# Reordering the first loads of a sketched-attention and four-expert kernel: keys in two runs a row, values in eight pieces, expert weights and query rows moved between them

## The chip, the cores and the metric

One core of a Trainium2 chip. A time is the device time in microseconds (us) of one execution; a kernel's time is the median of its runs. Every run in this study was in the fast state. A profile is of one of those runs, and its span is about 1.8 us shorter than the time of the same run (485.9 against 487.64 for the kernel before).

## The reference, cut to what matters

Attention with sketched keys and queries (each row is multiplied with two 8 x 32 matrices S1 and S2, and the products of the two results are its features), then four experts over every row.

```python
def phi(x):                                   # q, k, v: (4, 4, 1088, 32)
    a = np.einsum('rd,bhsd->bhsr', S1, x)     # S1, S2: (8, 32)
    b = np.einsum('rd,bhsd->bhsr', S2, x)
    return np.einsum('bhsi,bhsj->bhsij', a, b).reshape(*x.shape[:-1], 64)

q_p, k_p = phi(q), phi(k)
kv = np.einsum('bhsf,bhsd->bhfd', k_p, v)     # needs ALL keys and values of a batch
z = np.sum(k_p, axis=2)
out = einsum(q_p, kv) / (einsum(q_p, z) + 1e-06)
x = out as (4352, 128)
y = sum over e of p[:, e] * (relu(x @ w1[e]) @ w2[e])   # w1: (4,128,1024), w2: (4,1024,128)
```

The dependence that matters here: no attention output, and so no expert matmul, before the sum over all keys and values of batch 0 is complete, the last value tile included.

## The kernel before

Each DMA here is one load. `load_rows` fetches rows of k or q as 128 partitions, `load_v` fetches the values in four pieces of 32 partitions and then the 33rd and 34th rows (the "last value tile", two loads of 16 KB).

```python
def load_v(b):
    t = lpool.tile([P, H * NT * D], F32, tag="vn", name="vn")
    ...
    for a in range(4):                        # 4 x 128 KB, 32 partitions each
        nc.sync.dma_start(_ap(t, 32 * a, 32, 0, [[8 * D, H], [1, 8 * D]]), ...)
    for a in range(2):                        # the last value tile: 2 x 16 KB
        nc.sync.dma_start(_ap(t, 32 * a, 32, 1024, [[D, H], [1, D]]), ...)
    return t
...
load_rows(k, 0, "kn")                         # 544 KB, one load
load_rows(q, 0, "qn", slice(0, P))            # 64 KB
vn[0] = load_v(0)
...
load_rows(q, 0, "qn", slice(P, S))            # 480 KB
load_w1(0)                                    # 512 KB
# ... gate rows (dp, ends), w2(0), then w1 and w2 of experts 1 to 3
...
keep_warm(11)                                 # matmuls on constants, 0.43 us apart
```

In the part of `start` that the argument needs, ScalarE copies the values into the layout of the sums (`vx`), tile after tile, and only then copies `qb`, which the query products need:

```python
def value_copy(b):
    for r in range(2):
        nc.scalar.copy(vx[:, 4*r : 4*r+4, ...], _ap(vn[b], 0, P, P * r, ...))
        yield
    nc.scalar.copy(vx[0:64, 8, :, 0:D], _ap(vn[b], 0, 64, 1024, ...))   # the last tile

# in start():
    key_project(b, 0, kf[0]); key_project(b, 1, kf[1])
    next(value)
    key_project(b, 2, kf[2])
    for _ in value:                           # second copy, then the last tile
        pass
    ...
    nc.scalar.copy(qb[:, 0:n], fq[0][:, 0:n])
    # key products, key sums, query products, kvz, attention of the first rows, experts
```

Two facts count later, and the trace of the kernel before shows both. Only eight loads are under way at once: each load waits for the landing of the load eight before it in program order (the rest of q was issued at 4.95, the keys, eight loads before it, had landed at 4.93). And ScalarE runs its copies in program order (the second copy of values at 8.56, the last tile's at 9.09, qb's at 9.29).

Of the kernel before, what the change touches and what calls it, by code (L numbers as in the profile page):

```python
# [8 lines left out]
F32 = mybir.dt.float32  # L9
# [3 lines left out]
ACTF = mybir.ActivationFunctionType  # L13
# [3 lines left out]
def _ap(t, p0: int, np_: int, off: int, free):  # L17

    p = list(t.ap)[0]
    return bass.AP(t.tensor, t.offset + p0 * p[0] + off, [[p[0], np_]] + [list(d) for d in free])  # L20
# [3 lines left out]
def kernel(  # L24
# [24 lines left out]
    nc = tc.nc  # L49

    P = 128
    HP = 64
    B, H, S, D = q.shape
    E, DM, F = w1.shape
    R = 8
    R2 = 2 * R
    G = S // 32
    assert (B, H, S, D) == (4, 4, 1088, 32) and (E, DM, F) == (4, P, 1024)
    NT = 9
# [6 lines left out]
    UNITS = [[P, 448, 512], [512, 320, 256], [448, 512, P], [384, 320, 384]]  # L66
# [6 lines left out]
    cpool = ctx.enter_context(tc.tile_pool(name="const", bufs=1))  # L73
    lpool = ctx.enter_context(tc.tile_pool(name="loads", bufs=1))
# [9 lines left out]
    def psum(pool, tag):  # L84
        return pool.tile([P, 512], F32, tag=tag, name=tag)


    def load_rows(src, b, name, part=slice(0, S)):

        d = kn if name == "kn" else qn  # L90
        if b not in d:
            d[b] = lpool.tile([P, S], F32, tag=name, bufs=2, name=name)
        c, n = part.start, part.stop - part.start
        base = src.offset + b * H * S * D
        if name == "qn" and b == B - 1:
            for c, n, t in ((0, (G - 4) * D, 0), ((G - 4) * D, 4 * D, S - P)):
                nc.sync.dma_start(d[b][:, c : c + n], bass.AP(src.tensor, base + t * D, [[S * D, H], [n, 32], [1, n]]))
        else:
            nc.sync.dma_start(d[b][:, part], bass.AP(src.tensor, base + c, [[G * D, P], [1, n]]))

    def load_v(b):
        t = lpool.tile([P, H * NT * D], F32, tag="vn", name="vn")
        base = v.offset + b * H * S * D
        for a in range(4):
            nc.sync.dma_start(
                _ap(t, 32 * a, 32, 0, [[8 * D, H], [1, 8 * D]]),
                bass.AP(v.tensor, base + 8 * a * D, [[G * D, 32], [S * D, H], [1, 8 * D]]),
            )
        for a in range(2):
            nc.sync.dma_start(  # L110
                _ap(t, 32 * a, 32, 1024, [[D, H], [1, D]]),
                bass.AP(v.tensor, base + (32 + a) * D, [[G * D, 32], [S * D, H], [1, D]]),
            )
        return t

    kn, qn, vn = {}, {}, {}

    def load_batch(b):
        load_rows(k, b, "kn")
        vn[b] = load_v(b)  # L120
        load_rows(q, b, "qn")

    s_raw = cpool.tile([R2, 2 * D], I32, name="s_raw")
# [5 lines left out]
    def load_w1(e):  # L129
        nc.sync.dma_start(w1_sb[:, e, :], w1[e])  # L130

    def load_w2(e):
        nc.sync.dma_start(w2_sb[:, e], w2[e].rearrange("(f p) d -> p f d", p=P))

    load_rows(k, 0, "kn")
    load_rows(q, 0, "qn", slice(0, P))
    vn[0] = load_v(0)


    warm = nc.const_aps.tensor(1.0, (P, 512), BF16)  # L140

    idle = cpool.tile([P, 1], F32, name="idle")
    nc.scalar.activation(idle[:, :], nc.const_aps.tensor(1.0, (P, 1), F32), ACTF.Identity)
    dp = cpool.tile([P, G, E], F32, name="dp")

    ends = cpool.tile([P, 2, E], F32, name="ends")
    e_sum = cpool.tile([P, 2, 3], F32, name="e_sum")
    load_rows(q, 0, "qn", slice(P, S))
    load_w1(0)
    for p0, n, g0, m, t in ((0, 96, 0, G, 0), (96, 32, 0, G - 4, 3 * S), (96, 32, G - 4, 4, B * S - P)):  # L150
        nc.sync.dma_start(
            _ap(dp, p0, n, g0 * E, [[1, m * E]]),
            bass.AP(domain_probs.tensor, domain_probs.offset + t * E, [[m * E, n], [1, m * E]]),
        )
    for i, t, g in ((0, 0, G), (1, B * S - P, 4)):
        nc.sync.dma_start(
            ends[:, i, :], bass.AP(domain_probs.tensor, domain_probs.offset + t * E, [[g * E, 32], [1, 4 * E]])
        )
    load_w2(0)
    for e in range(1, E):  # L160
        load_w1(e)
        load_w2(e)
    sk = cpool.tile([P, P], F32, name="sk")
# [22 lines left out]
    def keep_warm(n):  # L186

        for _ in range(n):
            wp = psum(ps_h, "h")
            nc.tensor.matmul(wp[:, :], warm[:, 0:P], warm[:, :], start=True, stop=True)  # L190

    keep_warm(11)


    turn = [0]
# [130 lines left out]
    def key_turn(b, r, t0=0, n=4):  # L326
        if r < 2:
            nc.vector.transpose(  # L328
                _ap(kT, 0, P, 512 * r + P * t0, [[P, n], [32, 4], [1, 32]]),
                _ap(kn[b], 0, P, P * r + 32 * t0, [[32, n], [8 * D, 4], [1, 32]]),  # L330
            )
        else:
            nc.vector.transpose(kT[:, 1024:S], kn[b][:, 1024:S])
# [98 lines left out]
    def keys(b):  # L432
        for r in range(3):
            key_turn(b, r)
            yield
        kf = []
        for gi, (pool, tag) in enumerate(((ps_f, "f"), (ps_n, "den"), (ps_n, "num"))):
            kf.append(psum(pool, tag))
            key_project_wide(b, gi, kf[gi])
            if gi:  # L440
                key_add(b, gi - 1, kf[gi - 1])
            yield
        for _ in value_copy(b):
            pass
        for t0, n in ((0, 4), (4, 5)):
            if t0:
                key_add(b, 2, kf[2])
            for p in range(2):
                for x in range(2):
                    key_product(b, t0, n, p, x, nc.vector)  # L450
# [3 lines that stand above are left out]
        kv = psum(ps_f, "f")  # L454
        for p in range(2):
            key_sum(b, p, kv)
            yield
        key_blocks(b, kv)
        yield
# [214 lines left out]
    def start():  # L674
# [4 lines left out]
        for t0 in (0, 2):  # L679
            key_turn(b, 0, t0, 2)  # L680
        for r in (1, 2):
            key_turn(b, r)
# [52 lines left out]
    def front():  # L735
        for b in range(B):
            if b:
                yield from keys(b)
                if b + 1 < B:
                    load_batch(b + 1)  # L740
            c = 0
            for n in UNITS[b]:
                if b or c:
                    yield from queries(b, c, n)
                c += n
# [230 lines left out]
    for i in range(len(steps) + LA):  # L976
        if i < len(steps):
# [21 lines left out]
            if i == 2:  # L999
                gate_quotients()  # L1000
            elif i == 5:
                store_gates()
                load_gate(1)
                load_gate(2)
                load_batch(1)
# [43 lines left out]
```

## Time and profile before

| | kernel before |
|---|---|
| median time | 488.02 us (487.82 to 488.66, 3 runs) |
| span of the profile | 485.9 us |
| TensorE busy | 99% |
| first expert matmul (moment F) | 13.2 us |
| last piece of v landed | 7.66 us |
| last value tile landed | 8.06 us |
| w1 of expert 0 landed | 11.20 us |

Landings are read from the trace's DMA records; a load has landed when the last of its engines has finished. The kernel is bound by TensorE from F to the end (busy for 469.70 of the 469.70 us from 13.16 to 482.86), so the only time to be had is in front of F. The prediction below shows the lines for that. One line is added, because the explanation will rest on it: the stretch from 5 to 8 us, in which the values come in. Columns: stretch, length, busy time and count of TensorE, weight loads, VectorE, ScalarE and GpSimd, then granted clock, DMA share, GB/s.

```profile
5.00:8.00 3.00, 2.64 (x80) 2.48 (x81) 2.40 (x7) 1.40 (x5) 1.45 (x5) 1.00 1.02 229
```

The DMA engines are busy all through (share 1.02), at 229 GB/s.

### The profile page before, as it was taken

How to read it: one execution, taken by the hardware profiler on the slowest of the kernel's cores; microseconds unless marked ns; L12 is line 12 of the kernel's file. 1: busy time of each engine (PE TensorE's matmuls, PEld its weight loads, DVE VectorE, ACT ScalarE, POOL GpSimd, SP SyncE). 2: the span in 40 equal slices, each digit the busy share in tenths (PEclk: the TensorE clock that was granted, in tenths of full speed). 3: DMA queues.
4: the chain of work that ended last, by engine and by line, in shares of the span. 5: the costliest groups of instructions: out<-in, count | busy, mean ns of one | idle time of the engine just before them, and what ended most of it. 6: DMA issues, size and time to landing. Idle time of an engine off the chain costs nothing.

```text
span 485.9 us, 11377 instructions
## 1 busy us (share of the span) xinstructions
PE 481.5 (99%) x4551; PEld 362.7 (75%) x4551; DVE 320.9 (66%) x759; ACT 246.8 (51%) x496; POOL 230.0 (47%) x270
## 2 busy tenths in 40 slices
PE   8999999999999999999999999999999999999997
PEld 6965666667777777777777777677777777999997
DVE  6859675686766668486776757668684666665642
ACT  4354564445544555355445555445455555566651
POOL 5172654435444455415455444424555445555571
PEclk9999999999999999999999999999999999999999
DMA  7990050211003123031103100021101200120001
GB/s 223 278 299 10 23 150 12 88 20 45 2 9 106 24 69 93 2 89 20 40 1 130 24 12 1 3 86 24 34 0 56 50 1 0 45 55 4 15 1 20
DMA packets 37772, 26.25 MB, mean 54 GB/s; under 512 B 24824, under 2 KB 34520, under 8 KB 37208
## 3 DMA queue, kind: packets, MB, share of 16 engines
q1 hardware_dynamic: 37704, 25.53, 18.9%
q8 instruction: 36, 0.59, 0.5%
q14 instruction: 16, 0.13, 0.1%
q10 hardware_dynamic: 16, 0.00, 0.0%
HBM read 21.28 MB, written 4.24 MB: 53 GB/s over the span
## 4 chain that ended last, share of the span: by engine, by line
PE 97%; DMA 1%; DVE 1%; issue 0%; SPq 0%; ACT 0%; ACTq 0%
PE h L202 50%; PE o L202 41%; PE f L202 3%; PE den L202 2%; DMA kn<-in_k_dram 1%; PE num L202 1%; DVE qp L501 0%; DVE kp L391 0%; DVE kT L328 0%; DVE qT L488 0%; SPq L125 0%; DVE end L856 0%; DVE kvz L414 0%; ACT fs L360 0%; ACT vx L337 0%
## 5 line engine op out<-in xcount | busy, mean ns | idle before, releaser
L202 PE MATMUL h<-xT,w_sb 128*64 128x512 f32 (+5 forms) x1424 | 300.2, 491 | 0.0
L786 DVE SCALAR_TENSOR_TENSOR hid<-h,hid 128x256 f32<-128x256 f32 (+6 forms) x432 | 203.7, 472 | 143.3 <-ACT hid L817 134.9
L817 ACT ACTIVATE hid<-h 128x512 f32<-128x512 f32 (+3 forms) x288 | 158.5, 550 | 192.3 <-PE h L202 146.2
L202 PE MATMUL o<-hid,w2s 128*64 128x256 f32 (+3 forms) x1152 | 224.0, 355 | 0.0
L202 PEld LDWEIGHTS h<-xT,w_sb 128*64 128x64 f32 x1424 | 147.5, 137 | 50.4 <-issue 6.4
L202 PE MATMUL o<-hid,w_sb 128*64 128x256 f32 (+3 forms) x864 | 183.7, 355 | 0.0
L202 PEld LDWEIGHTS o<-hid,w2s 128*64 128x64 f32 x1152 | 132.2, 137 | 28.9
L930 POOL TENSOR_TENSOR ev<-yz,sh 64x256 f32<-64x256 f32 (+3 forms) x72 | 48.7, 676 | 159.9 <-ACT sh L933 157.2
L202 PEld LDWEIGHTS o<-hid,w_sb 128*64 128x64 f32 x864 | 100.5, 137 | 25.2 <-issue 5.8
L918 POOL TENSOR_TENSOR yz<-ev 128x512 f32<-128x512 f32 (+3 forms) x36 | 41.7, 1160 | 60.4 <-ACT ev L921 60.2
L930 POOL TENSOR_TENSOR ct<-ev 128x512 f32<-128x512 f32 (+3 forms) x36 | 42.5, 1182 | 2.8
L930 POOL TENSOR_TENSOR total<-total,ct 128x512 f32<-128x512 f32 (+3 forms) x27 | 31.9, 1181 | 2.1
L930 POOL TENSOR_TENSOR ct<-ct,gate 128x512 f32<-128x512 f32 (+3 forms) x27 | 31.8, 1177 | 2.1
L501 DVE TENSOR_TENSOR qp<-qa,qb 64x512 f32<-64x512 f32 (+5 forms) x44 | 30.1, 685 | 1.0
L920 ACT COPY ev<-o 128x512 f32<-128x512 f32 (+3 forms) x36 | 19.4, 539 | 12.7 <-PE o L202 12.3
L202 PE MATMUL o<-w_sb,hid 128*64 128x128 f32 x256 | 22.3, 273 | 0.0
L921 ACT COPY ev<-o 128x512 f32<-128x512 f32 (+3 forms) x36 | 19.4, 539 | 2.0
L202 PEld LDWEIGHTS o<-w_sb,hid 128*64 128x64 f32 x256 | 18.1, 137 | 1.6 <-issue 0.9
L809 ACT ACTIVATE hid<-h 128x256 f32<-128x256 f32 x23 | 8.4, 384 | 18.3 <-PE h L202 17.9
L391 DVE TENSOR_TENSOR kp<-fs 128x256 f32<-128x256 f32 (+1 forms) x24 | 16.6, 696 | 0.1
L933 ACT COPY sh<-yz 64x256 f32<-64x256 f32 (+3 forms) x36 | 13.7, 380 | 1.7 <-POOL yz L918 0.8
L202 PEld LDWEIGHTS den<-kvx,qp 128*64 128x64 f32 x240 | 12.5, 137 | 2.5 <-issue 0.5
(129 smaller groups left out, 247.5 us busy)
## 6 DMA issues: line engine op xcount, KB each, us to landing
w_sb<-in_moe_w_dram SPq DMA_DIRECT2D x8, 512.0 KB, 5.8
gate<-gates SPq DMA_DIRECT2D x4, 1024.0 KB, 4.7
kn<-in_k_dram SPq DMA_DIRECT2D x4, 544.0 KB, 7.0
vn<-in_v_dram SPq DMA_DIRECT2D x16, 128.0 KB, 3.5
gate<-gates SPq DMA_DIRECT2D x2, 896.0 KB, 6.4
qn<-in_q_dram SPq DMA_DIRECT2D x2, 544.0 KB, 4.0
out_dram<-ob SPq DMA_DIRECT2D x16, 64.0 KB, 2.0
qn<-in_q_dram SPq DMA_DIRECT2D x2, 480.0 KB, 5.0
```

Of the source, the lines that this page charges most:

```text
L202: nc.tensor.matmul(out(s), weights(s), moving(s), **flags)
L391: eng.tensor_tensor(out=_ap(kps[b], 0, P, 256 * t0 + P * p + 64 * x, [[256, n], [32, 2], [R, 4], [1, R]]), in0=_ap(src, 0, P, off + 4 * x, ...
L501: nc.vector.tensor_tensor(out=qp[p][64 * x : 64 * x + 64, 0:n], in0=qa[64 * p : 64 * p + 64, 0:n], in1=qb[64 * p : 64 * p + 64, 0:n], op=A ...
L786: nc.vector.scalar_tensor_tensor(out=out, in0=src, scalar=0.0, in1=in1, op0=ALU.max, op1=ALU.subtract)
L809: nc.scalar.activation(hd[:, 0 : 2 * n], hp[:, 0 : 2 * n], ACTF.Relu)
L817: nc.scalar.activation(hd[:, n * j : n * j + n], hp[:, 0:n], ACTF.Relu)
L918: add = lambda out, in0, in1, op=ALU.add: nc.gpsimd.tensor_tensor(out=out, in0=in0, in1=in1, op=op)
L920: nc.scalar.copy(_ap(ev, 0, P, 0, [[2 * w, 2], [1, w]]), _ap(a0, 0, P, 0, two))
L921: nc.scalar.copy(_ap(ev, 0, P, w, [[2 * w, 2], [1, w]]), _ap(a1, 0, P, 0, two))
L930: add = lambda out, in0, in1, op=ALU.add: nc.gpsimd.tensor_tensor(out=out, in0=in0, in1=in1, op=op)
L933: nc.scalar.copy(sh[HP:P, 0:w], yz[0:HP, 0, 0:w])
```

## The change

Intent: let the first half of the keys land early so that TensorE starts on them sooner; cut the values so that the first half of every row lands first; issue two of the loads from ScalarE; and fetch the first experts' weights sooner, as they are wanted next. All arithmetic stays the same. The core of the diff:

```diff
-    load_rows(k, 0, "kn")
-    load_rows(q, 0, "qn", slice(0, P))
-    vn[0] = load_v(0)
+    for part in (slice(0, 512), slice(512, S)):
+        load_rows(k, 0, "kn", part)               # 256 KB, 288 KB
+    v_tile(0)
+    for a in range(4):
+        load_v(0, 0, a)                           # 64 KB each
+    load_rows(q, 0, "qn", slice(0, P), nc.scalar) # issued by ScalarE
+    load_v(0, 1, 0, nc.scalar)                    # issued by ScalarE
+    for a in range(1, 4):
+        load_v(0, 1, a)
+    load_w1(0)
+    load_rows(q, 0, "qn", slice(P, P + UNITS[0][1]))   # 448 columns, 224 KB
+    load_v_end(0)                                 # the last value tile
+    load_w2(0)
...
-    load_rows(q, 0, "qn", slice(P, S))
-    load_w1(0)
     # ... dp
+    load_w1(1)
     # ... ends
-    load_w2(0)
-    for e in range(1, E):
+    load_w2(1)
+    load_rows(q, 0, "qn", slice(P + UNITS[0][1], S))
+    for e in range(2, E):
...
-    keep_warm(11)
+    keep_warm(9)
...
-                _ap(kn[b], 0, P, P * r + 32 * t0, [[32, n], [8 * D, 4], [1, 32]]),
+                _ap(kn[b], 0, P, 512 * r + 32 * t0, [[32, n], [P, 4], [1, 32]]),
```

The last hunk reads the keys in another order, so that the first half of the key tiles needs only the first run. The sum over keys does not care about the order, but values must follow it: that is why v is cut in eight.

More of the change, by code (lines that the diff above doesn't have):

```diff
@@ L85, in psum, with load_rows @@
         return pool.tile([P, 512], F32, tag=tag, name=tag)
-    def load_rows(src, b, name, part=slice(0, S)):
+    def load_rows(src, b, name, part=slice(0, S), engine=nc.sync):
         d = kn if name == "kn" else qn
@@ L98, in load_rows, with v_tile, load_v, load_v_end @@
         else:
-            nc.sync.dma_start(d[b][:, part], bass.AP(src.tensor, base + c, [[G * D, P], [1, n]]))
-    def load_v(b):
-        t = lpool.tile([P, H * NT * D], F32, tag="vn", name="vn")
-        base = v.offset + b * H * S * D
-        for a in range(4):
-            nc.sync.dma_start(
-                _ap(t, 32 * a, 32, 0, [[8 * D, H], [1, 8 * D]]),
-                bass.AP(v.tensor, base + 8 * a * D, [[G * D, 32], [S * D, H], [1, 8 * D]]),
-            )
+            engine.dma_start(d[b][:, part], bass.AP(src.tensor, base + c, [[G * D, P], [1, n]]))
+    def v_tile(b):
+        vn[b] = lpool.tile([P, H * NT * D], F32, tag="vn", name="vn")
+    def load_v(b, r, a, engine=nc.sync):
+        engine.dma_start(
+            _ap(vn[b], 32 * a, 32, P * r, [[8 * D, H], [1, P]]),
+            bass.AP(v.tensor, v.offset + (b * H * S + 16 * r + 4 * a) * D, [[G * D, 32], [S * D, H], [1, P]]),
+        )
+    def load_v_end(b):
         for a in range(2):
             nc.sync.dma_start(
-                _ap(t, 32 * a, 32, 1024, [[D, H], [1, D]]),
-                bass.AP(v.tensor, base + (32 + a) * D, [[G * D, 32], [S * D, H], [1, D]]),
+                _ap(vn[b], 32 * a, 32, 1024, [[D, H], [1, D]]),
+                bass.AP(v.tensor, v.offset + (b * H * S + 32 + a) * D, [[G * D, 32], [S * D, H], [1, D]]),
             )
-        return t
     kn, qn, vn = {}, {}, {}
@@ L119, in load_batch @@
         load_rows(k, b, "kn")
-        vn[b] = load_v(b)
+        v_tile(b)
+        for r in range(2):
+            for a in range(4):
+                load_v(b, r, a)
+        load_v_end(b)
         load_rows(q, b, "qn")
@@ L133, in load_w2 @@
         nc.sync.dma_start(w2_sb[:, e], w2[e].rearrange("(f p) d -> p f d", p=P))
-    load_rows(k, 0, "kn")
-    load_rows(q, 0, "qn", slice(0, P))
-    vn[0] = load_v(0)
-    warm = nc.const_aps.tensor(1.0, (P, 512), BF16)
     idle = cpool.tile([P, 1], F32, name="idle")
     nc.scalar.activation(idle[:, :], nc.const_aps.tensor(1.0, (P, 1), F32), ACTF.Identity)
+    for part in (slice(0, 512), slice(512, S)):
+        load_rows(k, 0, "kn", part)
+    v_tile(0)
+    for a in range(4):
+        load_v(0, 0, a)
[7 more added lines that the diff above has]
+    load_w2(0)
+    warm = nc.const_aps.tensor(1.0, (P, 512), BF16)
     dp = cpool.tile([P, G, E], F32, name="dp")
```

## The prediction

> **What bounds the kernel now.** I read the page's busy shares first, then the same shares cut into three stretches, then the chain of work that ended last for the first 14 us, then ScalarE's timeline there, then the DMA rates by microsecond.
>
> ```profile
> PE 481.5 (99%) x4551; PEld 362.7 (75%) x4551; DVE 320.9 (66%) x759; ACT 246.8 (51%) x496; POOL 230.0 (47%) x270
> ```
>
> TensorE is the engine that sets the end. Whether it ever waits is seen from the stretches (us, length, then busy time and count of PE, PEld, DVE, ACT, POOL, granted clock, DMA share, GB/s):
>
> ```profile
> 0.00:13.16 13.16, 11.83 (x195) 7.81 (x196) 8.74 (x37) 5.11 (x14) 7.42 (x35) 1.00 0.80 236
> 13.16:482.86 469.70, 469.70 (x4358) 354.90 (x4356) 311.82 (x722) 241.66 (x482) 222.62 (x236) 1.00 0.18 49
> 482.86:485.90 3.04, 0.00 (x1) 0.00 (x0) 0.35 (x1) 0.00 (x0) 0.00 (x0) 0.99 0.07 22
> ```
>
> From 13.16 us, the first matmul of the experts on the first 128 rows, TensorE is busy 469.70 of 469.70 us. So only two things are to be had: the 13.16 us before it (call that moment F) and the 3.04 us after it. The change touches only what comes before F and the later loads. A microsecond won or lost at F is a microsecond at the end, and nothing else counts unless a new wait appears later. All of F is 2.7% of 485.9 us, so a gain of 2% would need three quarters of the front to vanish.
>
> The chain of waits in the front (start, length, what):
>
> ```profile
> 1.21 3.72 DMA kn<-in_k_dram
> ...
> 5.55 2.10 PE h L202 x64
> ...
> 8.46 0.22 ACT fs L360
> ...
> 10.86 0.45 DVE qT L488
> ...
> 11.34 0.30 DVE kvz L414
> ...
> 12.34 0.89 PE o L202 x4
> 13.23 0.79 PE h L202 x21
> ```
>
> Keys load until 4.93, are transposed, projected for 2.1 us, multiplied out on VectorE, summed against the values (kvz needs that sum), and then attention for the first unit gives F. ScalarE in between copies the values and the query projection, one after the other in program order:
>
> ```profile
> 8.56 0.64 ACT L337 COPY vx<-vn 128x512 f32<-128x512 f32 x1
> 9.09 0.30 ACT L342 COPY vx<-vn 64x128 f32<-64x128 f32 x1
> 9.29 0.26 ACT L698 COPY qb<-o 128x128 f32<-128x128 f32 x1
> ```
>
> The reader is to see that qb, which the query products need, stands behind the copy of the last value tile (line 342). The products start at 9.64, run 1.19 us, then the qT transpose 0.45 us, and only then kvz at 11.34. VectorE has little slack there: its key products end at 9.73. Anything that holds the copy of line 342 past 9.09 moves F one for one.
>
> DMA in the front, by microsecond:
>
> ```profile
> 3.00:4.00 1.00, 1.00 (x4) 0.31 (x3) 0.93 (x7) 0.00 (x0) 0.22 (x2) 1.00 0.89 356
> 5.00:6.00 1.00, 0.64 (x16) 0.48 (x17) 1.00 (x3) 0.70 (x2) 0.70 (x3) 1.00 1.09 228
> 8.00:9.00 1.00, 1.00 (x23) 1.00 (x21) 0.72 (x3) 1.00 (x4) 0.71 (x2) 1.00 1.03 404
> ```
>
> The 16 DMA engines are already full (share about 1). Keys move at 356 GB/s, the values (pieces of 32 partitions) at 228 and then 182 in the next microsecond, queries and w1 at 404. So what is asked for first delays what is asked for next.
>
> [...] 228 and 182 GB/s for value pieces of 32 partitions, against 356 and 404. Cutting v into eight pieces of 32 partitions keeps that rate. [...] In the trace the loads of the SP queue land in the order of issue (k 4.93, q 5.26, the fourth v piece 7.7, the rest of q 9.9, w1 11.2). So a small load behind two big ones waits for both. [...] the 11 warming matmuls of 512 columns start 0.43 us apart, and the first 64 key matmuls take 2.10 us, 33 ns each for 64 columns.
>
> **The change, part by part.** I compared the built programs' order: on PE (apart from two warming matmuls), DVE and POOL the instructions stand as before, on ACT too except for two DMA issues. All of the effect is in when data lands.
>
> Keys in two runs. A count of bytes: 144 GB/s in 2-3 us and 356 in 3-4 put k's 557 kB through by 4.17 us, and it landed 0.76 us later. The first run, 262 kB, is through at 3.0 + 118/356 = 3.33, and lands at about 4.1. VectorE ends its work on S1 and S2 at 4.04 and the copies into sk end at 4.59, so neither holds it. First matmul of the keys: 4.1 + 0.46 + 0.14 = about 4.7, against 5.55, a gain of 0.85. Nine warming matmuls instead of eleven end 0.86 us earlier, at about 4.6, just out of the way.
>
> The second run cannot land before k did, 4.93, [...]: say 5.1. Its transpose (0.67) ends at 5.77 plus 0.14; TensorE is through the first 32 matmuls at 4.7 + 1.05 = 5.75. That gives back about 0.15, leaving 0.7.
>
> Values in eight pieces. Same bytes, same 32 partitions each. The first four (and one of the second four, from ScalarE's queue), 328 kB at the mean of 228 and 182, land at 5.2 + 1.6 = 6.8. The first copy of values, 7.94 before, would come at 7.2, so it does not wait; with v as before (whole pieces, the last at 7.7) it would have. The last of the eight lands as before, 7.7; the second copy, 8.56 before, is due at 7.9. Up to here 0.7 us are won.
>
> The last value tile (two loads of 16 KB, the 34th rows). It now stands behind w1 of expert 0 (524 kB) and 448 columns of q (229 kB). Issue first: SP holds at most eight loads in flight, the next issue waits for the landing eight before (the rest of q is issued at 4.95, right after k's 4.93; w1 at 5.41 after q's 5.26). In the new order the seventh v piece waits for k's second run, 5.1, and then, at about 0.45 us per issue, come another v piece (5.55), w1 (6.0), q (6.5), the tile (6.95 and 7.4). So w1's data, about 1 us after issue, cannot begin before 7.0 [...]. From landing to landing: 7.7 (v) + 1.3 (w1, as 9.9 to 11.2 before) + 0.57 to 0.86 (229 kB at 404 GB/s, or at the slower rate of q's 492 kB before, about 1.85 us) + 0.3 (two small loads, estimate) = 9.9 to 10.2; with no gap anywhere, 9.4. The copy of line 342, at 9.09 before, then starts at about 9.9, qb at 10.1, the query products at 10.45, kvz at 12.15, F at 13.96. The 0.7 us won are spent in ScalarE's wait and 0.8 us are lost.
>
> Weights and gates. In the old order w1 of expert 1 lands at 9.93 + 5.2 = 15.1 and is needed at 15.87: covered. In the new order w1 and w2 of experts 0 and 1 land sooner, those of 2 and 3 have the same bytes ahead as before. TensorE never waited for them, so sooner wins nothing by itself; it only makes room for an earlier F. The gates' rows land a little later, about 14, and VectorE takes their sums at 16.4. Four more v issues in each of three later loads of a batch cost SP 4 x 0.43 = 1.7 us at a time; the next batch is needed tens of us later.
>
> Sum: +0.8 us at F by the working, so 488.8.
>
> **The rivals.** (a) The last tile lands early enough, below about 8.3, and F moves up by the full 0.7 to 0.85: 487.2. For it: that is what the order was made for, two fewer warming matmuls fit it exactly, and a tuner would keep only an order that helped. Against it: 1.9 MB stand ahead of that tile, which from 2.2 us on at an unbroken 404 GB/s is 6.9 us and a landing near 9.4. (b) My working, the wait moves to the last tile: 488.4 to 489.1. (c) Half and half: [...] v speeds up to about 300 GB/s and ends 0.6 us earlier, the tile lands at 9.3: 488.2. (d) [...] the key matmuls run at half clock: up to 2 us more; or a later xT is late behind eight v issues. Each under one in twenty.
>
> **Range and chances.** I give (b) 0.6, (c) 0.2, (a) 0.15. The middle is 488.5. Runs of the old kernel spread from 487.82 to 488.66, so I add 0.3 on each side of 487.3 to 489.0. Two per cent is 9.8 us, which no path above reaches.
>
> **What would show it.** The first key matmul at about 4.7 (first step). No wait for v in the first copy of values. ScalarE idle before the copy of line 342's counterpart, ended by a load of vn, and that copy starting near 9.9; VectorE idle before the query products (second step, the one that decides). F near 13.9, and TensorE again without a gap to its end, 469.7 us later. If that copy starts by 8.3, [...] (a) is right; if TensorE shows gaps after F, weights or later loads bind and the whole argument from F falls.

## The result, and the profile after

| | before | after |
|---|---|---|
| median time, measured side by side | 488.17 us (487.53 to 488.67, 6 runs) | 491.25 us (490.44 to 493.17, 6 runs) |
| span of the profile | 485.9 us | 488.8 us |
| F, from the chain of waits | 13.23 us | 16.58 us |

The ratio is 1.0067 (95% interval 1.0045 to 1.0088): within 2%, but a loss of about 3.3 us, and outside the predicted range. Ratios, here and below, are the mean time of one kernel's fast runs over that of the other's fast runs of the same rounds, so they are not quite the ratio of the medians.

The chain of waits of the changed kernel (start, length, what), from the keys to the first expert matmul:

```profile
1.62 4.14 DMA kn<-in_k_dram
...
5.78 0.31 SPq L105
6.09 0.04 issue
6.13 0.43 SPq L105
6.57 0.04 issue
6.61 0.44 SPq L135
7.05 0.04 issue
7.09 0.43 SPq L99
7.52 0.04 issue
7.57 0.43 SPq L112
8.00 0.04 issue
8.04 4.43 DMA vn<-in_v_dram
12.47 0.02 issue
12.49 0.30 ACT vx L359
12.79 0.17 ACT qb L715
...
14.68 0.30 DVE kvz L431
...
15.69 0.89 PE o L219 x4
16.58 1.57 PE h L219 x48
```

In the kernel before, this chain went from the keys' load over TensorE, ScalarE and VectorE. Here it goes over none of them until 12.49. It starts with the keys' second run, then follows SP's queue: two pieces of v (line 105), w1 (135), the query columns (99), the last value tile (112), one issue after another. Then it waits 4.43 us for that last tile. From there the steps to F are the old ones: 4.09 us from the tile's copy to F, against 4.14 before (9.09 to 13.23).

ScalarE's timeline of the changed kernel says the same from the waiting side:

```profile
8.72 0.64 ACT L354 COPY vx<-vn 128x512 f32<-128x512 f32 x1
12.49 0.30 ACT L359 COPY vx<-vn 64x128 f32<-64x128 f32 x1 [3.13 <-DMA vn<-in_v_dram]
12.69 0.25 ACT L715 COPY qb<-o 128x128 f32<-128x128 f32 x1
```

The bracket is the idle time and what ended it: 3.13 us, a load of vn. The second copy of values, at 8.56 before, starts at 8.72; the last tile's copy, at 9.09 before, starts at 12.49. VectorE stands behind it:

```profile
12.98 0.59 DVE L518 TENSOR_TENSOR qp<-o,qb 64x128 f32<-64x128 f32 x2 [3.10 <-ACT qb L715]
```

The longest wait of SP for a load in the first 16 us of the changed kernel:

```profile
SPq L105 <- DMA kn<-in_k_dram: 1.3, 1, 1.3
```

SP was held for 1.3 us before the seventh piece of v, because eight loads were under way: the keys' second run was done on 15 engines at 5.01 and on the last at 5.76. The DMA rates of the changed kernel, in the same columns as above:

```profile
5.00:6.00 1.00, 1.00 (x32) 0.98 (x30) 0.22 (x1) 0.70 (x2) 0.77 (x3) 1.00 0.93 158
6.00:7.00 1.00, 0.48 (x17) 0.39 (x14) 1.00 (x4) 0.37 (x1) 0.33 (x1) 1.00 0.17 45
...
8.00:9.00 1.00, 1.00 (x23) 1.00 (x21) 0.56 (x2) 1.00 (x4) 0.09 (x1) 1.00 0.83 254
```

```profile
5.00:8.00 3.00, 2.48 (x76) 2.37 (x76) 1.67 (x5) 1.24 (x4) 1.97 (x5) 1.00 0.62 118
```

This is the answer to the 229 GB/s at a share of 1.02: from 5 to 8 us the changed kernel moves 118 GB/s at a share of 0.62, and from 6 to 7 us the engines are nearly idle (0.17). Bytes were wanted; what was lacking were loads that had been issued. How deep the hole is differs between executions: experiments 3 and 7 have the same loads in front, and their profiles show waits of 0.9 and 0.8 us there, and 163 and 150 GB/s from 5 to 8 us.

After F nothing is lost. TensorE in 60 to 485 us of the changed kernel:

```profile
60.00:485.00 425.00, 425.00 (x3794) 323.40 (x3792) 279.12 (x642) 219.75 (x433) 204.16 (x205) 1.00 0.14 38
```

From F to the end of the span the kernel before takes 485.9 - 13.23 = 472.7 us and the changed one 488.8 - 16.58 = 472.2. So the loss is all in front of F.

### The profile page after: what moved, and what is told of

Its sections match the earlier page's. It is cut to its first block, busy times and chain, and to the rows that moved or that the text cites. A ratio compares the mean times of both kernels' runs of the same rounds, so it can differ in the third digit from the quotient of the medians.

```text
span 488.8 us, 11401 instructions
## 1 busy us (share of the span) xinstructions
PE 481.5 (99%) x4549; PEld 362.9 (74%) x4549; DVE 320.6 (66%) x759; ACT 246.3 (50%) x496; POOL 229.8 (47%) x270
## 4 chain that ended last, share of the span: by engine, by line
PE 96%; DMA 2%; SPq 1%; DVE 0%; issue 0%; ACT 0%
PE h L219 49%; PE o L219 41%; PE f L219 3%; PE den L219 2%; DMA vn<-in_v_dram 1%; DMA kn<-in_k_dram 1%; PE num L219 1%; DVE qp L518 0%; SPq L99 0%; SPq L105 0%; DVE qT L505 0%; SPq L135 0%; SPq L112 0%; SPq L130 0%; DVE end L873 0%
## 5 line engine op out<-in xcount | busy, mean ns | idle before, releaser
L937 ACT COPY ev<-o 128x512 f32<-128x512 f32 (+3 forms) x36 | 19.4, 538 | 12.7 <-PE o L219 12.3
L219 PE MATMUL o<-w_sb,hid 128*64 128x128 f32 x256 | 21.1, 273 | 0.0
L219 PEld LDWEIGHTS o<-w_sb,hid 128*64 128x64 f32 x256 | 16.9, 137 | 1.6 <-issue 0.9
L219 PEld LDWEIGHTS f<-vx,kp 128*64 128x64 f32 x288 | 11.4, 137 | 4.1 <-ACT vx L359 2.2
```

The costliest lines, as they stand in the source:

```text
L219: nc.tensor.matmul(out(s), weights(s), moving(s), **flags)
L937: nc.scalar.copy(_ap(ev, 0, P, 0, [[2 * w, 2], [1, w]]), _ap(a0, 0, P, 0, two))
```

## The experiments

Three theories were set against each other at first. T: the last value tile's place, behind w1 and the query columns, holds ScalarE and with it F. R: something else in the front (a late second run of keys, or contention) would hold F near its new place even with the tile early. H, later: the granted clock falls in the long idle stretch (five of the changed kernel's six runs had a mean of 0.993 to 0.997) and that is the extra loss; what it costs was the author's estimate. Since T alone did not explain the size, two more were added: the eight small pieces leave the DMA engines without work (L), or it is the order in which the pieces of 32 partitions follow each other (P).

**1. The changed kernel with the last tile's loads ahead of w1.**

```diff
         load_v(0, 1, a)
+    load_v_end(0)
     load_w1(0)
     load_rows(q, 0, "qn", slice(P, P + UNITS[0][1]))
-    load_v_end(0)
     load_w2(0)
```

> The changed kernel with one edit: the two small loads of the last value tile stand right behind the eight pieces of v, ahead of w1 of expert 0. Theory T (the tile waits in its ring behind w1 and q, and ScalarE, VectorE and TensorE wait for it): the tile lands near 8.5 us instead of 12.47, ScalarE's copy of it starts near 9.2, F (first expert matmul) near 13.3 instead of 16.5, time 488.0 to 488.6, that is level with before. Rival R (the late second run of k, 5.76, which stalls the SP queue, is the loss, wherever the tile stands): F above 15 and 490 or more.

Measured: 489.33 us, ratio to the kernel before 1.0026 [1.0013, 1.0038]. The tile landed at 8.36 and its copy started where T put it:

```profile
8.69 0.30 ACT L359 COPY vx<-vn 64x128 f32<-64x128 f32 x1
```

But F came at 14.55, not at 13.3, and the time was above the expected 488.0 to 488.6. (The profiled run is the slowest of the five.) The chain of waits of this run shows a second late load behind the first:

```profile
7.48 4.66 DMA qn<-in_q_dram
...
12.16 0.45 DVE qT L505
...
14.55 2.74 PE h L219 x48
```

The 448 query columns stood behind w1 and landed at 12.14; VectorE has their transpose ahead of kvz in its order, so kvz waited. TensorE was busy for only 1.12 of the 3 us from 11 to 14. The granted clock was 0.56 in the stretch 14 to 17 us of this run and 0.87 in 17 to 20, and 48 expert matmuls took 2.74 us where the changed kernel, at a clock of 1.00, needed 1.57:

```profile
14.00:17.00 3.00, 3.00 (x52) 2.54 (x50) 2.79 (x10) 0.47 (x2) 0.72 (x4) 0.56 0.99 293
```

What follows: T holds (R falls, F was well below 15), but undoing the tile's place recovers only about 2.0 of the 3.3 us (1.0067 to 1.0026 of 488), because w1 ahead of the query columns hurts as well.

**2. The other way round: the kernel before with its last tile behind the rest of q and w1.**

```diff
         for a in range(4): ...
+        if b:
+            load_v_end(b, t)
...
     load_rows(q, 0, "qn", slice(P, S))
     load_w1(0)
+    load_v_end(0, vn[0])
```

> The kernel before with one edit: the last value tile's two loads stand behind the rest of q and w1 of expert 0; k in one load, v in four pieces, no load on ScalarE's queue but S1. T: the tile lands at 11.5 to 12.5, F at 15.7 to 16.5, time 490.7 to 491.5: this part alone makes the whole loss. R: no late k here, so no loss, 487.8 to 488.6.

Measured: 490.23 us, ratio 1.0038 [1.0025, 1.0052], less than the expected 490.7 to 491.5. The wait appears, and it is shorter (the profiled run, 488.96 us, is the fastest of the five):

```profile
10.78 0.30 ACT L348 COPY vx<-vn 64x128 f32<-64x128 f32 x1 [1.33 <-DMA vn<-in_v_dram]
```

The tile landed at 10.70, although w1 and 480 KB of q were issued ahead of it (in the changed kernel w1 and only 224 KB of q). So the place alone produces the wait and costs about 1.9 us (0.0038 x 488). It doesn't explain a landing of 12.47, and it does not make the whole loss, as had been expected.

**3. The changed kernel with ScalarE's copy of qb ahead of the last tile's copy.**

```diff
-        for _ in value:
-            pass
+        next(value)
         ...
         nc.scalar.copy(qb[:, 0:n], fq[0][:, 0:n])
+        for _ in value:
+            pass
```

> The changed kernel with the copy of qb ahead of the copy of the last value tile on ScalarE. T says part of the loss is ScalarE's order: VectorE makes its query products (1.2 us) and the transpose (0.45) while the tile is still on its way; after the tile's copy only TensorE's last sums (0.8) are left before kvz, so kvz comes near 13.6 to 13.8 instead of 14.68, F about 1.0 us earlier, near 15.5, time 490.2. If the order of the copies does not matter: 491.2 as changed.

Measured: 490.35 us, ratio 1.0045 [1.0033, 1.0058], about 1.1 us under the changed kernel, near the expected gain; but the two intervals overlap ([1.0045, 1.0088] there), so the gain is likely and not clear of noise. The query products no longer waited (qb at 9.07), and the tile held only the last key sums. The profiled run lost part of this to a lower clock (0.89 granted from 11 to 14 us, 0.54 from 14 to 17; the four matmuls ahead of F took 1.49 us, 0.89 in the changed kernel), so its F says little. If the 1.1 us stand, the order of ScalarE's copies is about a third of the loss, on top of a late tile.

**4. As experiment 1, with the one v piece that ScalarE issued given to SP.**

```diff
     load_rows(q, 0, "qn", slice(0, P), nc.scalar)
-    load_v(0, 1, 0, nc.scalar)
-    for a in range(1, 4):
+    for a in range(4):
         load_v(0, 1, a)
```

> As e1_tile_early, and the piece of v that went through ScalarE's queue back on SP's. Theory S (that piece overtakes the second run of k and holds its landing at 5.76): k's second run lands near 5.1, the second fs copy near 7.2 instead of 7.83, F near 12.7, time about 0.5 us below e1, 487.5 to 487.9. Rival (k in two runs of shorter rows is itself slower): second run stays near 5.7, time equal to e1.

Measured: 489.15 us, ratio 1.0032 [1.0018, 1.0045], no different from experiment 1 within its interval. F came at 13.8, not at the expected 12.7. The keys' second run landed at 5.10 here, at 5.20 in experiment 1 and at 5.76 in the changed kernel; as it moves by 0.5 us in kernels whose first loads are the same (5.16 in experiment 7, 5.30 in experiment 3), the piece from ScalarE can't be blamed for it. Inconclusive, and worth little.

**5. The changed order of loads, but v in four pieces of 128 KB.** The keys come in two runs of 512-byte rows that keep the old key order, so the values can stay whole; everything else is as in the changed kernel, the late tile included.

```diff
+    def load_key_runs(b):                       # strided runs: 4 x 512 B a row
+        for r in range(2):
+            nc.sync.dma_start(
+                _ap(kn[b], 0, P, P * r, [[8 * D, 4], [1, P]]),
+                bass.AP(k.tensor, base + P * r, [[G * D, P], [8 * D, 4], [1, P]]))
+        load_rows(k, b, "kn", slice(8 * P, S))
...
+    load_key_runs(0)
+    load_rows(q, 0, "qn", slice(0, P), nc.scalar)
+    vn[0] = load_v(0)                           # four pieces
+    load_w1(0)
+    load_rows(q, 0, "qn", slice(P, P + UNITS[0][1]))
+    load_v_end(0, vn[0])
+    load_w2(0)
```

> The changed kernel's order of loads (tile behind w1 and q), but v in four pieces of 128 KB and the keys' two runs cut so that they keep the old key order (rows of 512 B). Theory L (SP holds eight loads in flight; eight 64 KB pieces fill the eight places, SP stands still from about 4.4 to 5.8 us, [...] 118 GB/s in 5 to 8 us against 229 before): here 200 GB/s or more in 5 to 8 us, w1 issued before 5 us and landed near 10, the tile at 10.5 to 11.0, F 14.7 to 15.0, 489.2 to 489.9. Rival (the tile is late by its place alone): tile at 12 or later, 491.

Measured: 489.06 us, ratio 1.0029 [1.0017, 1.0041]. The stretch from 5 to 8 us and the last tile's copy:

```profile
5.00:8.00 3.00, 2.70 (x80) 2.73 (x82) 2.26 (x7) 1.57 (x5) 1.78 (x6) 1.00 1.04 225
```

```profile
11.13 0.30 ACT L360 COPY vx<-vn 64x128 f32<-64x128 f32 x1 [1.12 <-DMA vn<-in_v_dram]
```

With the same partitions and the same bytes, in pieces of twice the size, the engines are full again (1.04, 225 GB/s), w1 is issued at 4.70 in place of 6.61 and lands at 9.78 in place of 10.63, and the tile lands at 11.05 in place of 12.47. The ratio falls from 1.0067 to 1.0029: about 1.9 of the 3.3 us come with the eight small pieces, about 1.4 with the order of the loads. Of the 1.4 us between the two landings of the tile, 0.6 are there when the query columns have landed (10.57 against 11.16); the other 0.8 are one late engine in the tile's own loads, of which more below. The kernels also differ in the keys' rows (512 bytes a run in place of 2 KB), which experiment 8 tests by itself, and larger pieces of v have longer rows too (1 KB in place of 512 bytes); number of pieces and length of rows were not tested apart.

**6. Keys in two runs, v in four pieces, then the last tile, the query columns, and only then w1.**

```diff
     vn[0] = load_v(0)
-    load_w1(0)
-    load_rows(q, 0, "qn", slice(P, P + UNITS[0][1]))
     load_v_end(0, vn[0])
+    load_rows(q, 0, "qn", slice(P, P + UNITS[0][1]))
+    load_w1(0)
```

(shown against experiment 5; the first 128 query columns are issued by SP here)

> Keys in two runs, v in four pieces, then the tile, then 448 columns of q, then w1 and w2 of expert 0, all on SP. If the loss is the tile, the rows of q behind w1, and the eight places, all three are gone: tile near 8.1, q near 9.3, F near 12.9, no gap after F, clock 1.0, 487.4 to 488.2: level with or a little under before. If something else in the change costs time: 488.8 or more.

Measured: 488.19 us, ratio 1.0006 [0.9993, 1.0019]: within the noise the loss is gone, and nothing is won. The tile landed at 9.12, not near 8.1, and F was 14.10 in the profile, not near 12.9. The gain of the early keys is spent at once in a wait for the values:

```profile
8.82 0.63 ACT L355 COPY vx<-vn 128x512 f32<-128x512 f32 x1 [1.23 <-DMA vn<-in_v_dram]
```

The fourth piece landed at 8.75, against 7.66 in the kernel before. Keys that come earlier only bring the next wait to light: v must come with them.

**7. The changed kernel with ten more warming matmuls in its gap.**

```diff
                 key_sum(b, p, kv, t0, n0)
+            if t0 == 0:
+                keep_warm(10)
```

> The changed kernel with ten warming matmuls [...] where TensorE waits for the last tile. Theory H [...]: clock 1.0 in every run here, spread under 1 us, mean about 490.6, some 0.8 under the changed kernel's 491.4. Rival (the low clock falls where TensorE waits anyway): 491.3 as before.

Measured: 490.9 us, ratio 1.0067 [1.0055, 1.0079]. All six runs had a mean clock of 1.0 (four of the changed kernel's six had 0.996 or 0.997, and one 0.993), and the time was the same. The last tile was just as late:

```profile
12.48 0.30 ACT L359 COPY vx<-vn 64x128 f32<-64x128 f32 x1 [3.72 <-DMA vn<-in_v_dram]
```

The profile of the changed kernel itself has a clock of 1.0 throughout, and F at 16.58 all the same: the wait alone makes that delay. No gain from the steadier clock is seen; but the 0.8 us that H expected are 0.0016, inside what the two intervals leave open, so H is not needed, and a small part for it is not excluded.

This run says more, since its loads are those of the changed kernel. In its chain of waits w1 (line 135) was issued at 6.01, not at 6.61, and the tile came no sooner:

```profile
6.01 0.43 SPq L135
...
7.44 5.01 DMA vn<-in_v_dram
```

So the late second run of the keys, and the 0.6 us by which w1 was issued later for it, are not what made the tile late.

**8. The kernel before with only the keys cut into two runs** (with the small end and nine warming matmuls; all other loads in the old order).

```diff
-    load_rows(k, 0, "kn")
+    load_key_runs(0)                            # as in experiment 5
     load_rows(q, 0, "qn", slice(0, P))
     vn[0] = load_v(0)
```

> The kernel before with the keys in two runs (and a small end), nine warming matmuls, all other loads in the old order and sizes. First key matmul near 4.7 instead of 5.55; the first value copy then waits for v's fourth piece, 7.7; F 12.9 to 13.1, 487.6 to 488.1: the earlier keys alone are worth 0.1 to 0.3 us, since v stands close behind them. If earlier keys carry through: F near 12.4, 487.2.

Measured: 488.14 us, ratio 1.0009 [0.9997, 1.0021]. ScalarE's first copy of key projections began at 6.50 (6.73 before), the values landed later (8.09), F was 13.4, and TensorE had a new wait of 0.8 us for w1 of expert 1, which landed at 17.00 (15.2 before):

```profile
PE h L217 <- DMA w_sb<-in_moe_w_dram: 0.8, 1, 0.8
```

Early keys by themselves win nothing, and the strided runs cost nothing, that is clear of the noise.

**9. The kernel before with the four v pieces in the order 0, 64, 32, 96** (P).

```diff
-        for a in range(4):
+        for a in (0, 2, 1, 3):
```

> The kernel before with v's four pieces in the order of partitions 0, 64, 32, 96 instead of 0, 32, 64, 96. [...] 5 to 7 us at 260 GB/s or more, v's last piece at 7.2 or sooner instead of 7.7; F stays at 13.1, since keys bind there, 487.6 to 488.2. Rival (rate set by row size or by v being read in short rows): 205 GB/s and 7.7 as before.

Measured: 487.93 us, ratio 0.9996 [0.9983, 1.0009]. From 5 to 6 us 254 GB/s moved (228 before) and from 6 to 7 us 205 (182 before); the last piece landed at 7.55 in place of 7.66. That is less than the 260 GB/s and the 7.2 us expected. Experiment 2, with the old order of the pieces, had 235 GB/s from 5 to 6 us and the last piece at 7.79, so a part of the difference is spread between executions. In these single profiles the order of the pieces has at most a small part in the rate of these loads, and the time doesn't move. Why another order should be faster was the author's guess, and no run shows a cause.

**10. As experiment 4, with the query columns ahead of w1 too.** Everything that the front needs is now ahead of all weights.

```diff
+    load_v_end(0)
+    load_rows(q, 0, "qn", slice(P, P + UNITS[0][1]))
     load_w1(0)
-    load_rows(q, 0, "qn", slice(P, P + UNITS[0][1]))
     load_w2(0)
```

> e4 with the 448 columns of q also ahead of w1 of expert 0: the changed kernel with both of its late loads mended, eight pieces of v kept. In e4 the last waits were for q (landed 11.5) and for w1 of expert 2 (20.7). Here q near 9.4, F near 12.8, but the weights come as late as in e4 (SP issues one load in 0.45 us, 64 KB each: 145 GB/s in 5 to 8 us), so TensorE then waits about 1.5 us for w1 of expert 1 or 2: 487.8 to 488.6. If weights were no limit: 487.2, under before.

Measured: 488.75 us (487.84 to 490.7), ratio 1.0016 [0.9999, 1.0033]. The tile's copy started at 8.87 and F came near 13.2, as in the kernel before. But then TensorE waited for the weights, which it never did in the kernel before:

```profile
PE o L218 <- DVE qa L663: 2.3, 1, 2.3
...
PE h L218 <- DMA w_sb<-in_moe_w_dram: 0.5, 1, 0.5
```

The first line is an example of a releaser that the profile names wrongly: VectorE had long been done, and w2 of expert 1 landed only at 20.74. The second is w1 of expert 2 (22.77). In both loads a single engine was late: 15 of 16 had finished at 18.45 and at 20.96. So these waits are not shown to come from the eight pieces. (The profiled run was the slowest of the six, so they are the upper end.) None of the ten beats the kernel before; 6, 8, 9 and, just, 10 can't be told from it.

## Why the prediction was wrong

The mechanism was right, and the size wasn't: the prediction had +0.8 us at F and a range up to 489.3; measured were 491.25 us, F at 16.58 in the place of 13.96.

*Right: where to look.* TensorE again shows no gap after F, and all of the loss is in the front. Later loads never held TensorE in the changed kernel (busy for 468.42 of the 468.42 us from 16.58 to 485).

*Right: the keys.* First key matmul at 4.76, with about 4.7 worked out; the first copy of key projections at 6.16 (6.73 before). The 4.7 is partly luck: the first run landed at 3.80, not at 4.1, and the matmul then waited 0.9 us for GpSimd's copy of S1 and S2 into sk, which the working had said would not hold it. *Off:* the second run landed at 5.76, not at 5.1, and the head start was gone by the first copy of values (8.10, against 7.94 before and a predicted 7.2). That copy did not wait for v, as predicted.

*Right: the wait that decides.* ScalarE idle ahead of the last tile's copy, ended by a load of vn; VectorE idle ahead of the query products. Experiments 1 and 2 show it both ways. Rivals (a) and (c) are out. (The "landing near 9.4" under (a) does not follow from its numbers: 1.9 MB at 404 GB/s take 4.7 us, which from 2.2 us on end at 6.9. Nothing rests on it.)

*The step that failed* is the sum for the last tile, "7.7 (v) + 1.3 (w1 ...) + 0.57 to 0.86 (...) + 0.3 (two small loads, estimate) = 9.9 to 10.2". Term by term, from landing to landing, in the three profiles that have these loads:

| term | predicted | changed kernel | experiment 3 | experiment 7 |
|---|---|---|---|---|
| v, last piece | 7.7 | 8.12 | 7.74 | 7.65 |
| w1 of expert 0 behind v | 1.3 | 2.51 (10.63) | 2.75 (10.49) | 3.15 (10.80) |
| query columns behind w1 | 0.57 to 0.86 | 0.53 (11.16) | 0.63 (11.12) | 0.69 (11.49) |
| last tile behind them | 0.3 | 1.31 (12.47) | 1.09 (12.21) | 0.97 (12.46) |

The prediction went on with 9.9, the low end of its sum. The tile landed 2.6 us after that (2.3 and 2.6 us in the other two), and in the changed kernel F followed one for one, as it was said to. v and the query columns came out about right; the terms of w1 and of the tile did not.

*The term of w1.* The 1.3 us were not the time that w1 takes. They were what was left of it in the kernel before once q had landed. The traces' DMA records show w1 as the first 128 packets of 4096 bytes. In the kernel before, the first of them started at 8.04, and w1 landed 3.16 us later; 1.87 of these us passed while q was still landing (9.91), and 1.3 were left. In the changed kernel the first started at 7.68, about 1.1 us after the issue at 6.61, and w1 landed 2.95 us later; only 0.44 us of these lay before the end of v (8.12). In experiment 7 w1 was issued at 6.01, as predicted, and v landed at 7.65, as predicted; w1's first packet started at 7.10, and w1 still took 3.70 us. The prediction had worked out both, w1's issue at 6.0 and that its data "cannot begin before 7.0"; 7.0 and about 3 us (2.5 to 3.7 in the twelve profiles) make 10, not 9.0.

Why so little of w1 lay beside v is the part that the change made. A piece of 64 KB every 0.45 us is 65.5 kB / 0.45 us = 146 GB/s at best (an estimate from these traces), less than the 229 GB/s that the engines had taken, and the limit of eight stops the issue on top of it. So v's last pieces landed about as fast as they were issued, and w1 was issued only 0.48 us behind the last of them. Where the engines stayed full, the predicted terms about hold: in experiment 5, with pieces of 128 KB, w1's first packet started 2.1 us before v had landed, w1 landed 1.09 us behind v and the tile 0.48 behind the query columns; in experiment 2 w1 landed 1.41 us behind q and the tile 0.40 behind w1. The sentence that carried the mistake was "The 16 DMA engines are already full (share about 1)": it was true of the kernel before, and the change undid it (0.62 from 5 to 8 us). That eight pieces keep the rate of 228 and 182 GB/s was likewise the author's estimate; measured were 158, 45 and 150 GB/s in the three microseconds from 5 to 8.

The traces put the size of a piece and the rate side by side: 118, 163 and 150 GB/s from 5 to 8 us with pieces of 64 KB (the changed kernel, experiments 3 and 7), 229 and 225 with 128 KB (the kernel before, experiment 5). An issue took about 0.45 us, and 64 KB at the 229 GB/s of the kernel before would take 0.29 (an estimate).

*The term of the last tile* was mis-sized by 0.7 to 1.0 us. In the changed kernel its first load was done on its first engine at 10.49, on its fifteenth at 11.34 and on its last at 12.22. Why one engine was that far behind is not shown. The traces have a candidate. In this kernel's trace one packet of 16 KB, of the kind "instruction" on queue q8, runs from 9.97 to 10.98 us; the DMA view from 9.9 to 11.1 us has it (packets, MB, share of the 16 engines):

```profile
q8 instruction: 1, 0.02, 5.3%
```

In experiment 5 such a packet came at 10.74, when the tile was nearly through, and the load that had one engine late, by 1.1 us, was the next one, w2. The records do not name the engine, and no run tested it. The small load was as late as its slowest engine (12.22, when the fifteenth was done at 11.34): its size got it no discount here.

Rival (d), the clock, did show up, in this kernel's other runs (a mean of 0.993 to 0.997) and in the profiles of experiments 1 and 3 (0.56 and 0.54 from 14 to 17 us), though there behind the key matmuls; the delay of F is there at a granted clock of 1.00 too (16.58 in the profile).

Open: what holds the one late engine; whether the number of pieces or the length of their rows counts; what the lower clock costs in experiments 1 and 3, where it couldn't be taken out alone; and why F to the end varies by up to 0.8 us (472.7 before, 471.9 in experiment 5), so that experiment 5's F, 2.0 us later than before, cost only 1.4.

## What to carry to other kernels

When a change cuts loads smaller, ask first whether the issuing queue can still keep the DMA engines busy: piece size over issue time is a rate (here 64 KB in 0.45 us, 146 GB/s), and where the number of loads under way is limited (eight here), smaller loads reach it after fewer bytes (SP was held for 1.3 us). Don't carry the time "from one landing to the next" from a profile with full engines into an order in which they may run dry: look up when the load's first packet started, and how much of it was hidden behind the load in front (w1 was put at 1.3 us and took 2.95 from its first packet). And follow the smallest load that a long chain of work needs: behind two big ones it decided the front here (its copy at 12.49 in place of 9.09), whatever the big ones gained.
